# In the middle of a long convolution, GpSimd folds products that TensorE summed, and the last routing steps move

## The chip, the core and the metric

The kernel runs on one core of one Trainium2 chip. A core has TensorE (matmuls into PSUM), VectorE, ScalarE and GpSimd (elementwise work; GpSimd reaches SBUF only) and SyncE, called SP, which here only issues DMAs. The metric is the time of one execution on the device in microseconds, the median of three runs.

## The reference

A gated long convolution over 4 sequences ("blocks" below) of 11456 tokens and 128 channels, then a mixture of 8 experts, each token sent to one of them.

```python
h_filt = (np.maximum(pos_emb @ w1, 0.0) @ w2) * np.exp(-0.01 * pos)[:, None]
y = irfft(rfft(x * v, 2 * S) * rfft(h_filt, 2 * S))[:, :S]   # causal convolution along the sequence
x = (x * y).reshape(B * S, D)
logits = x @ w_gate + modality_bias[modality_id]
e_idx = np.argmax(logits, axis=1)
gate_w = softmax(logits)[np.arange(N), e_idx]
out[mask] = gate_w[mask, None] * (np.maximum(x[mask] @ w1[e], 0.0) @ w2[e])   # for each expert e
```

## The kernel before

**The convolution** is a two-step transform. After the filter has been transformed once (its spectra go to DRAM as `hs`), each of the four blocks has an *outer stage* and a *middle*. The outer stage of block b has 16 steps: it multiplies x by v and transforms them (forward), and for block b - 1 it does the inverse transform, the multiplication by x, and the routing: logits, `choice` (maximum, exponential, first best expert as a one-hot array `oh` and its running count `sc`), and `send`, which in spite of its name makes only the ranks (row numbers `ix` within each expert's region) from matmuls of `oh` and `sc`. Routing goes in octets `o` of 0 to 7, one every two steps. `store` writes an octet's finished rows from SBUF (`xo`) to DRAM (`xr`), two DMAs of 365.6 KB on SP; `places` writes the row numbers once all are known.

**The middle** of a block has 23 groups of four rows of the spectrum, `A` (the last has two). For group g, `spectrum` is TensorE's second transform (line 602) into a pair of PSUM banks, of which there are two; `products` has VectorE multiply it with the filter's spectra: two half-size products into `more` (line 619), two full ones into `part` (line 626). GpSimd combines `more` (lines 621, 622); one subtraction on `part` (line 630, GpSimd up to group 4, VectorE after) and one addition (line 631, GpSimd) follow. `inverse` sums on TensorE, for its two output blocks: two terms of `p` (which is `part[0]`) for block 0, and the same two and two of `more` for block 1 (line 650). ScalarE copies the result into `A`. Two groups go together: spectrum and products of groups 2k and 2k + 1, and then the inverse of the pair before. SP loads for each group its constants `c_b` (for `spectrum`) and `c_c` (for `inverse`) and the spectra `hs`, into rings of three places; a load waits until its place has been read.

**The order** of instructions on TensorE, ScalarE, VectorE and SP is that of the program; `steps` builds lists of steps, and `joined` writes out by hand how the end of an outer stage goes over into the middle. In its list, `mid[0]` has groups 4 and 5 (spectrum, products), `mid[1]` the inverse of 2 and 3, `mid[2]` groups 6 and 7, and so on; each step also holds the loads of one group. SP is such a queue, too: a DMA that waits holds up all that are written behind it. GpSimd's order is left to the framework's planner.

**Rows sent.** Each row of a routed block must go to its expert's region in DRAM, `xs`. `fetch` (SP) loads a block's row numbers, and `send_rows(n)` sends n columns of 128 rows by indirect DMAs of GpSimd (line 267); every fifth column needs a load of rows on ScalarE's queue. A block has 90 columns. They are sent in the outer stages (`paced`: after an instruction of VectorE), in the middles, and among the expert tiles.

**The experts.** 82 tiles of 512 rows and 22 of 256 follow (of the last five, only as many as are needed), with two matmul layers in chunks of 128 hidden channels, each in three matmuls of split precision; GpSimd scatters the results (line 1216).

Of the kernel before, what the change touches and what calls it, by code (L numbers as in the profile page):

```python
# [33 lines left out]
PU = 64 + HALF  # L34
# [4 lines left out]
NG = -(-N1 // G)  # L39
# [138 lines left out]
def hyena_moe_kernel(ctx: ExitStack, tc: tile.TileContext, a: dict, out: bass.AP,  # L178
# [46 lines left out]

    scatters, waiting, finale = [], [], []
    order_dep = mybir.DependencyInfo(mybir.DependencyClass.NoSync, mybir.DependencyReason.DATA)
# [25 lines left out]
    def fetch(b):  # L253
# [3 lines left out]
        waiting.extend((b, c) for c in range(NR // D))  # L257

    def send_rows(n, behind=None, wait=None):


        for _ in range(min(n, len(waiting))):
            b, c = waiting.pop(0)
            if c % RC == 0:
                rows_back(b, c // RC + 1, act)
            ix, src = to_t[b % 2][:, c:c + 1], back_t[(b * NB + c // RC) % 3][:, c % RC]
            s = pool.indirect_dma_start(  # L267
                out=xs, out_offset=bass.IndirectOffsetOnAxis(ap=ix, axis=0), in_=src,
                in_offset=None, bounds_check=E * R - 1, oob_is_err=False)
            free_rows(scatters, s)  # L270
            if behind is not None:
                tc.add_manual_dep(ins_of(s), behind.name, order_dep, reason="order of issue")
            if wait is not None:
                tc.add_manual_dep(ins_of(s), wait.name, sync_dep, reason="pace")
# [85 lines left out]
    with ExitStack() as cv:  # L360
# [80 lines left out]
        def forward_stages(b):  # L441
# [7 lines left out]
            def product(q):  # L449

                u = kept[q, "u"]
                s = dve.tensor_mul(u, u, kept.pop((q, "v")))
                paced(s, 2)

# [116 lines left out]
        def middle_stages(b):  # L571
# [36 lines left out]
            def products(g):  # L608
# [13 lines left out]
                pool.tensor_add(more[:, 0, 1], more[:, 0, 1], more[:, 1, 0])  # L622
                if g == 6 and b > 0:
                    fetch(b - 1)
                for i in range(2):
                    dve.tensor_mul(  # L626
                        part[i], z[:, :, i].unsqueeze(1).broadcast_to([D, 2, n, 2, D]),
                        h[:, 0].unsqueeze(3).broadcast_to([D, 2, n, 2, D]))
                p = part[0]
                (pool if g <= 4 else dve).tensor_sub(p[:, 0], p[:, 0], part[1][:, 1])  # L630
                s = ins_of(pool.tensor_add(p[:, 1], p[:, 1], part[1][:, 0]))  # L631
                if 4 < g < NG - 2:
                    send_rows(1 + (g % 3 == 0), s)
                k["p"], k["m"] = p, more[:, 0]

            def inverse(g):
# [4 lines left out]
                for q in range(n):  # L641
                    for blk in range(2):
                        terms = [(p[:, c, q, blk], c) for c in range(2)]
                        if blk:
                            terms += [(more[:, c, q], c) for c in range(2)]
                        for i, (t, c) in enumerate(terms):
# [18 lines left out]
        def inverse_stages(b):  # L665
# [15 lines left out]
            def transform(q):  # L681
# [3 lines left out]
                for c in range(2):  # L685
                    for blk in range(2):
# [7 lines left out]
                paced(dve.tensor_mul(xo_of(b, q // 2)[:, :, q % 2, :, 0:D], four(y),  # L694
                                     four(kept.pop(q))))

# [14 lines left out]
        def route_stages(b):  # L711
# [55 lines left out]
            def choice(o):  # L767
                i = b * NO + o
                xo = xo_of(b, o)
                lg = kept.pop(o)  # L770
# [5 lines left out]
                act.activation(ex[:, 0:E], dl, AF.Exp)  # L776
                oh, sc = oh_t[i % 2], sc_t[i % 2]
                sco = score[0:PU]
                dve.scalar_tensor_tensor(sco[:, 0:E], dl, 0.0, fst, op0=ALU.is_ge, op1=ALU.mult)
                mb = rt.tile([PU, NC], F32, tag="mb", name="mb")  # L780
                dve.tensor_reduce(mb, ec(sco), axis=AX.X, op=ALU.max)
                dve.tensor_tensor(oh[0:PU], sco[:, 0:E], wide(mb), op=ALU.is_equal)
                dve.tensor_tensor_scan(
# [36 lines left out]
            def places(o):  # L820
                if o == NO - 1:
                    for blk in range(2):
                        at = xi[b].rearrange("(k n x) -> k n x", k=2, n=HALF)
                        sp.dma_start(at[blk], ix_all[64 * blk:64 * blk + HALF].rearrange("p w m -> p (w m)"))

            return turn, logits, logits_turn, shift, biased, choice, send, store, places

# [6 lines left out]
        def outer_steps(b):  # L834
# [3 lines left out]
            if b > 0:  # L838
                load_x, turn, itransform = inverse_stages(b - 1)
                rturn, logits, lturn, shift, biased, choice, send, store, places = route_stages(b - 1)  # L840
                todo = {
# [24 lines left out]
            if 0 < b < nb:  # L866
                for name in ("half", "logits", "lturn", "shift", "biased", "choice", "send", "store", "places"):
                    later[b, name] = lambda f=todo[name]: f(NQ - 1)
                    todo[name] = but_last(todo[name], 1)
                todo.pop("places")  # L870
# [8 lines left out]
        def joined(b, seq):  # L879
# [5 lines left out]
            if b == 0:  # L885
# [9 lines left out]
                    + do("shift", "half", "products0", "spectrum1", "logits", "load_h2", "load3",  # L895
                         "products1", "spectrum2", "lturn", "load_c1", "products2",
                         "inverse0", "load4", "load_c2", "spectrum3", "biased", "choice",
                         "inverse1", "load5", "load_c3", "store", "products3")
                    + mid[:1] + do("send") + keep + mid[1:2] + do("places") + mid[2:])

# [117 lines left out]
    def experts(lo, hi):  # L1018
# [209 lines left out]
        for at in range(len(work) + 6):  # L1228
# [8 lines left out]
            if lo == 0 and at >= FL + len(finale) + 2 and len(waiting) <= RC and not fetched:  # L1237
                fetched.append(fetch(nb - 1))
            if lo == 0 and at % 3 == 0:
                send_rows(1)  # L1240
# [66 lines left out]
```

## Time and profile before

| | |
|---|---|
| median of 3 runs | 2106.36 us (2105.53 to 2107.07) |
| the profiled execution | 2104.89 us, span 2102.7 us |
| busy share of the span | TensorE 97%, VectorE 80%, GpSimd 60%, ScalarE 57% |
| mean granted clock of TensorE | 0.992 of full speed |

In the profile PE is TensorE, PEld its weight loads, DVE VectorE, ACT ScalarE, POOL GpSimd, and SPq the DMA issues of SP; a line number is that of the kernel. The span goes from the first to the last instruction. The filter and the first forward stage take the first 149 us, the middles lie at 149 to 257, 382 to 496, 622 to 736 and 861 to 975 us, the outer stages between them and until 1062, and the experts after that. Busy shares are means over these stages; what bounds a stage is read from its own rows.

### The profile page before, as it was taken

To read this page: it belongs to the slowest core of one execution; us is meant where nothing else is said; L and a number is where in the kernel's file an instruction comes from. 1 tells how busy PE (TensorE), PEld (TensorE's weight loads), DVE (VectorE), ACT (ScalarE), POOL (GpSimd) and SP (SyncE) were. 2 spreads that over 40 slices of the span, in tenths; PEclk is the share of its full clock that TensorE was granted. 3 is DMA by queue.
4 is the path that set the end of the run, shared out by engine and by line. 5 is a ranking of instruction groups with operands and counts; after the bars stand their busy time and mean duration, and the time that the engine had idled before them with its cause. 6 is when DMAs were issued, how large, how long until landed. Compare 5 with 4: busy or idle time off the path is not lost. (4 is left out here: it accounts for less than half of the span.)

```text
span 2102.7 us, 50304 instructions
## 1 busy us (share of the span) xinstructions
PE 2037.7 (97%) x18162; PEld 1671.1 (79%) x18162; DVE 1680.5 (80%) x2692; ACT 1191.8 (57%) x2162; POOL 1251.2 (60%) x1337
## 2 busy tenths in 40 slices
PE   8989999899999999899999999999999999999996
PEld 8888877688767877687668888888888888888896
DVE  2348767896779867897887899988989999899885
ACT  4642266225652266324666666666666666666674
POOL 0207500597658866687746667777876465555553
PEclk9999999999999999999999999999999999999998
DMA  9577777687888789785798455665665554454310
GB/s 322 222 275 239 250 222 248 201 288 282 294 279 262 257 288 318 254 270 189 216 279 256 89 122 121 131 137 120 135 132 111 110 107 99 94 100 97 78 41 26
DMA packets 509590, 397.55 MB, mean 189 GB/s; under 512 B 372697, under 2 KB 406317, under 8 KB 509337
## 3 DMA queue, kind: packets, MB, share of 16 engines
q1 hardware_dynamic: 472889, 312.26, 53.1%
q0 software_dynamic: 26496, 59.36, 7.9%
q10 hardware_dynamic: 9952, 22.67, 3.8%
q8 instruction: 145, 2.38, 0.5%
q14 instruction: 108, 0.88, 0.1%
HBM read 290.58 MB, written 103.96 MB: 188 GB/s over the span
## 5 line engine op out<-in xcount | busy, mean ns | idle before, releaser
L1167 DVE SCALAR_TENSOR_TENSOR hl<-ph,hh 128x512 fp32r<-128x512 f32 x724 | 485.5, 680 | 101.2 <-ACT hh L1166 93.7
L1166 ACT ACTIVATE hh<-ph 128x512 fp32r<-128x512 f32 x724 | 425.1, 598 | 213.7 <-PE ph L1163 203.2
L267 POOL DMA_INDIRECT xs<-back,to x360 | 388.0, 1078 | 184.8 <-issue 65.5
L1216 POOL DMA_INDIRECT out<-ot,idx x362 | 395.0, 1091 | 140.4 <-issue 112.2
L1163 PE MATMUL ph<-xl,wh 128*128 128x512 f32 (+1 forms) x792 | 296.4, 374 | 4.5 <-DVE xl L1148 4.4
L1161 PE MATMUL ph<-xh,wh 128*128 128x512 f32 (+1 forms) x792 | 298.8, 377 | 1.1 <-ACT xh L1147 1.1
L1162 PE MATMUL ph<-xh,wl 128*128 128x512 f32 (+1 forms) x792 | 294.8, 372 | 1.0 <-DVE wl L1116 1.0
L1184 PE MATMUL po<-hh,wh 128*128 128x512 f32 (+1 forms) x792 | 294.8, 372 | 0.0
L1186 PE MATMUL po<-hl,wh 128*128 128x512 f32 (+1 forms) x792 | 294.3, 372 | 0.0
L1185 PE MATMUL po<-hh,wl 128*128 128x512 f32 (+1 forms) x792 | 294.0, 371 | 0.0
L655 ACT COPY A<-pw 128x512 f32<-128x512 f32 x180 | 96.0, 584 | 328.9 <-PE pw L650 328.9
L626 DVE TENSOR_TENSOR part<-pz,rings 128x1024 f32<-128x1024 f32 (+1 forms) x184 | 211.5, 1189 | 2.5 <-POOL part L631 2.5
L650 PE MATMUL pw<-rings,part 64*128 64x128 f32 x2880 | 200.6, 278 | 1.4 <-ACT A L655 1.4
L650 PEld LDWEIGHTS pw<-rings,part 64*128 64x128 f32 x2880 | 179.3, 190 | 19.7 <-issue 14.8
L602 PE MATMUL pz<-A,rings 128*64 128x256 f32 x1440 | 172.1, 389 | 18.9 <-issue 14.5
L464 PE MATMUL s<-fwd,seq 128*64 128x90 f32 x4096 | 170.8, 243 | 5.9 <-issue 4.2
L1163 PEld LDWEIGHTS ph<-xl,wh 128*128 128x128 f32 x792 | 149.6, 189 | 33.0 <-DVE xl L1148 5.8
L464 PEld LDWEIGHTS s<-fwd,seq 128*64 128x64 f32 x4096 | 161.3, 137 | 13.2 <-issue 4.9
L1162 PEld LDWEIGHTS ph<-xh,wl 128*128 128x128 f32 x792 | 149.7, 189 | 26.4 <-DVE wl L1116 1.3
L1161 PEld LDWEIGHTS ph<-xh,wh 128*128 128x128 f32 x792 | 149.6, 189 | 26.0 <-ACT xh L1147 1.3
L1184 PEld LDWEIGHTS po<-hh,wh 128*128 128x128 f32 x792 | 149.2, 188 | 26.0 <-issue 0.7
L1186 PEld LDWEIGHTS po<-hl,wh 128*128 128x128 f32 x792 | 149.2, 188 | 25.8
(191 smaller groups left out, 3606.8 us busy)
## 6 DMA issues: line engine op xcount, KB each, us to landing
rings<-hs SPq DMA_DIRECT2D x88, 512.0 KB
seq<-in_u SPq DMA_DIRECT2D x64, 512.0 KB
seq<-in_v SPq DMA_DIRECT2D x64, 512.0 KB
seq<-in_x SPq DMA_DIRECT2D x64, 512.0 KB
xr<-xo SPq DMA_DIRECT2D x64, 365.6 KB
rings<-in_c_b SPq DMA_DIRECT2D x88, 256.0 KB
rings<-in_c_c SPq DMA_DIRECT2D x88, 256.0 KB
back<-xr ACTq DMA_DIRECT2D x68, 325.0 KB
```

The source lines that it names most:

```text
L267: s = pool.indirect_dma_start(out=xs, out_offset=bass.IndirectOffsetOnAxis(ap=ix, axis=0), in_=src, in_offset=None, bounds_check=E * R - 1 ...
L464: pe.matmul(v[64 * c:64 * c + 64, blk, j], u[:, blk, 4 * h + j], fwd[:, c], start=True, stop=True)
L650: pe.matmul(pw[par][:, to:to + D], t[at], k["c"][at, q, c], start=i == 0, stop=i == len(terms) - 1)
L1161: pe.matmul(p, k[0, "h"][:, f:f + D], k["xh"], start=True, stop=False)
L1162: pe.matmul(p, k[0, "l"][:, f:f + D], k["xh"], start=False, stop=False)
L1163: pe.matmul(p, k[0, "h"][:, f:f + D], k["xl"], start=False, stop=True)
L1166: act.activation(hh, ph, AF.Relu)
L1167: dve.scalar_tensor_tensor(hl, ph, 0.0, hh.bitcast(F32), op0=ALU.max, op1=ALU.subtract)
L1184: pe.matmul(po, k[1, "h"][:, f], hh[:, t], start=g == 0, stop=False)
L1185: pe.matmul(po, k[1, "l"][:, f], hh[:, t], start=False, stop=False)
L1186: pe.matmul(po, k[1, "h"][:, f], hl[:, t], start=False, stop=g == NCH - 1)
L1216: s = pool.indirect_dma_start(out=out, out_offset=bass.IndirectOffsetOnAxis(ap=k["idx"][:, j:j + 1], axis=0), in_=ot[:, j, :], in_offset=N ...
```

## The change

- **Fold.** In groups 4 to 19 of block 0 and 10 to 19 of the other blocks, GpSimd adds `more[:, 0, 0]` to the block-1 half of `p[:, 0]` (256 elements a partition), and `inverse` leaves that term out. The last three groups and the first ones are not folded.
- **Who subtracts.** GpSimd does the subtraction on `part` in the first groups (below 4 in block 0, below 10 in the others) and in even groups up to 18; VectorE in the rest.
- **Rows.** The middle sends no rows any more, but for two after its last group. A block's `fetch` is made at group 15 or by `send_rows`, as soon as the block is stored and no more than five columns wait. In exchange every second `product` sends a column more, and every second `inverse` of the last outer stage; among the expert tiles one goes out in every second chunk of the first 12 tiles and then in three of eight.
- **The last two octets' routing.** The ranks of octet 6 move from the end of the outer stage to the place ahead of `mid[0]`. `choice` of octet 7 is split into `best` (maximum, difference, exponential, first best) behind `mid[0]`, and `chosen` (one-hot array, counts, gate) behind `mid[2]`; `store` follows `chosen`; the ranks of octet 7 come behind `mid[4]`, and `places` behind `mid[5]`. `biased` and the products of group 3 move ahead.

```diff
+    def fetch_next():
+        if stored and len(waiting) <= RC:
+            fetch(stored.pop(0))
     def send_rows(n, behind=None, wait=None):
+        fetch_next()
...
-                paced(s, 2)
+                paced(s, 2 + (q % 2 == 0))
...
-                if g == 6 and b > 0:
-                    fetch(b - 1)
+                if g == NG - 8:
+                    fetch_next()
...
-                p = part[0]
-                (pool if g <= 4 else dve).tensor_sub(p[:, 0], p[:, 0], part[1][:, 1])
-                s = ins_of(pool.tensor_add(p[:, 1], p[:, 1], part[1][:, 0]))
-                if 4 < g < NG - 2:
-                    send_rows(1 + (g % 3 == 0), s)
-                k["p"], k["m"] = p, more[:, 0]
+                p, early, late = part[0], g < (4 if b == 0 else 10), g >= NG - 3
+                by_pool = early or (g % 2 == 0 and not late)
+                (pool if by_pool else dve).tensor_sub(p[:, 0], p[:, 0], part[1][:, 1])
+                pool.tensor_add(p[:, 1], p[:, 1], part[1][:, 0])
+                k["p"], k["m"] = p, {c: more[:, 0, c] for c in range(2)}
+                if not early and not late:
+                    pool.tensor_add(p[:, 0, :, 1], p[:, 0, :, 1], k["m"].pop(0))
+                if g == NG - 1:
+                    send_rows(2)
...
-                            terms += [(more[:, c, q], c) for c in range(2)]
+                            terms += [(m[:, q], c) for c, m in more.items()]
...
-                                     four(kept.pop(q))))
+                                     four(kept.pop(q))), 1 + (b == nb - 1 and q % 2))
...
             def choice(o):
+                best(o)
+                chosen(o)
...
+                    if b < nb - 1:
+                        stored.append(b)
...
-                    todo[name] = but_last(todo[name], 1)
+                    todo[name] = but_last(todo[name], 3 if name == "send" else 1)
+                later[b, "ranks"] = lambda: send(NO - 2)
+                later[b, "best"], later[b, "chosen"] = lambda: best(NO - 1), lambda: chosen(NO - 1)
...
-                         "products1", "spectrum2", "lturn", "load_c1", "products2",
-                         "inverse0", "load4", "load_c2", "spectrum3", "biased", "choice",
-                         "inverse1", "load5", "load_c3", "store", "products3")
-                    + mid[:1] + do("send") + keep + mid[1:2] + do("places") + mid[2:])
+                         "products1", "spectrum2", "lturn", "load_c1", "biased", "products2",
+                         "inverse0", "load4", "load_c2", "spectrum3", "products3",
+                         "inverse1", "load5", "load_c3", "ranks")
+                    + mid[:1] + do("best") + mid[1:3] + do("chosen", "store") + mid[3:5]
+                    + do("send") + keep + mid[5:6] + do("places") + mid[6:])
...
-            if lo == 0 and at % 3 == 0:
+            if lo == 0 and c % (2 if i < 12 else 3) == 0:
                 send_rows(1)
```

## Rows read from the trace of the kernel before

**Rows 1.** Stretches: length; busy PE, PEld, DVE, ACT, POOL; clock; DMA share; GB/s.

```profile
368.00:420.00 52.00, 45.87 (x567) 34.50 (x565) 42.49 (x71) 14.93 (x28) 26.06 (x30) 0.97 0.66 199
420.00:473.00 53.00, 53.00 (x738) 43.94 (x736) 50.33 (x60) 13.40 (x26) 49.47 (x53) 1.00 0.87 289
788.00:841.00 53.00, 53.00 (x704) 39.32 (x701) 38.02 (x74) 36.01 (x67) 34.23 (x37) 1.00 0.92 320
1200.00:1400.00 200.00, 200.00 (x884) 165.77 (x883) 180.67 (x279) 135.80 (x240) 146.89 (x152) 1.00 0.59 125
```

**Rows 2.** Timeline of PE, settled middle: start, us, instruction, idle before.

```profile
690.31 3.67 PE L602 MATMUL pz<-A,rings 128*64 128x256 f32 x32
...
695.36 1.06 PE L650 MATMUL pw<-rings,part 64*128 64x128 f32 x16
696.25 0.61 PE L650 MATMUL pw<-rings,more 64*128 64x128 f32 x8
696.69 1.06 PE L650 MATMUL pw<-rings,part 64*128 64x128 f32 x16
...
699.47 3.67 PE L602 MATMUL pz<-A,rings 128*64 128x256 f32 x32
```

**Rows 3.** Timeline of VectorE (DVE), settled middle.

```profile
705.66 1.28 DVE L619 TENSOR_TENSOR more<-pz,rings 128x512 f32<-128x512 f32 x2
...
709.23 0.69 DVE L630 TENSOR_TENSOR part<-part 128x512 f32<-128x512 f32 x1
```

**Rows 4.** Timeline of GpSimd (POOL) in early groups, where it sends no rows.

```profile
407.48 0.72 POOL L622 TENSOR_TENSOR more<-more 128x256 f32<-128x256 f32 x1
408.17 1.27 POOL L630 TENSOR_TENSOR part<-part 128x512 f32<-128x512 f32 x1
409.40 1.26 POOL L631 TENSOR_TENSOR part<-part 128x512 f32<-128x512 f32 x1
```

**Rows 5.** Groups by line, GpSimd, 170 to 250 us (block 0): busy, mean ns.

```profile
L631 POOL TENSOR_TENSOR part<-part 128x512 f32<-128x512 f32 x18 | 30.7, 1704 | 12.4 <-DVE part L626 12.3
```

**Rows 6.** Timeline of GpSimd among the expert tiles: two sends.

```profile
1303.45 0.98 POOL L267 DMA_INDIRECT xs<-back,to  x1 [0.30 <-issue]
1304.73 0.98 POOL L267 DMA_INDIRECT xs<-back,to  x1 [0.30 <-issue]
```

**Rows 7.** Timeline of PE, entry of the middle of block 1.

```profile
382.31 1.95 PE L602 MATMUL pz<-A,rings 128*64 128x256 f32 x16 [0.86 <-ACT A L467]
...
389.22 1.95 PE L602 MATMUL pz<-A,rings 128*64 128x256 f32 x16 [1.19 <-issue]
...
391.71 1.16 PE L650 MATMUL pw<-rings,part 64*128 64x128 f32 x16
...
404.29 2.69 PE L602 MATMUL pz<-A,rings 128*64 128x256 f32 x16 [3.00 <-issue]
...
407.25 1.87 PE L650 MATMUL pw<-rings,part 64*128 64x128 f32 x16
...
414.45 3.67 PE L602 MATMUL pz<-A,rings 128*64 128x256 f32 x32
```

**Rows 8.** Timeline of VectorE, entry of block 1: `biased`, and the products after `choice`.

```profile
395.95 0.29 DVE L764 TENSOR_TENSOR lg<-lt,lg 109x128 f32<-109x128 f32 x1
...
400.66 1.27 DVE L619 TENSOR_TENSOR more<-pz,rings 128x512 f32<-128x512 f32 x2
```

**Rows 9.** Timeline of SP's DMA issues, entries of blocks 1 and 3.

```profile
400.78 1.78 SPq L797 DMA_DIRECT2D xr<-xo  x2
402.66 1.56 SPq L577 DMA_DIRECT2D rings<-in_c_b  x1
...
899.11 0.43 SPq L577 DMA_DIRECT2D rings<-in_c_b  x1
```

**Rows 10.** Stretch behind that store in block 1, columns as in the first group.

```profile
402.00:407.00 5.00, 2.71 (x18) 1.60 (x19) 5.00 (x6) 0.00 (x0) 4.07 (x5) 0.84 0.82 201
```

**Rows 11.** Timeline of PE, entry of block 3.

```profile
905.12 1.95 PE L602 MATMUL pz<-A,rings 128*64 128x256 f32 x16 [0.99 <-DMA rings<-in_c_b]
```

More of the change, by code (lines that the diff above doesn't have):

```diff
@@ L224, in hyena_moe_kernel @@
     sc_t = [cst.tile([D, E, NC], BF16, name=f"sc{i}") for i in range(2)]
-    scatters, waiting, finale = [], [], []
+    scatters, waiting, finale, stored = [], [], [], []
     order_dep = mybir.DependencyInfo(mybir.DependencyClass.NoSync, mybir.DependencyReason.DATA)
@@ L767, in choice, with best @@
             def choice(o):
-                i = b * NO + o
-                xo = xo_of(b, o)
+                best(o)
+                chosen(o)
+            def best(o):
                 lg = kept.pop(o)
@@ L776, in choice @@
                 act.activation(ex[:, 0:E], dl, AF.Exp)
-                oh, sc = oh_t[i % 2], sc_t[i % 2]
                 sco = score[0:PU]
@@ L781, in choice, with chosen @@
                 dve.tensor_reduce(mb, ec(sco), axis=AX.X, op=ALU.max)
+                kept[o] = mb
+            def chosen(o):
+                i = b * NO + o
+                xo = xo_of(b, o)
+                mb = kept.pop(o)
+                ex, sco = powers[0:PU], score[0:PU]
+                oh, sc = oh_t[i % 2], sc_t[i % 2]
                 dve.tensor_tensor(oh[0:PU], sco[:, 0:E], wide(mb), op=ALU.is_equal)
@@ L824, in places @@
                         sp.dma_start(at[blk], ix_all[64 * blk:64 * blk + HALF].rearrange("p w m -> p (w m)"))
-            return turn, logits, logits_turn, shift, biased, choice, send, store, places
+                    if b < nb - 1:
+                        stored.append(b)
+            return turn, logits, logits_turn, shift, biased, choice, send, store, places, best, chosen
         def every_other(f):
@@ L839, in outer_steps @@
                 load_x, turn, itransform = inverse_stages(b - 1)
-                rturn, logits, lturn, shift, biased, choice, send, store, places = route_stages(b - 1)
+                rturn, logits, lturn, shift, biased, choice, send, store, places, best, chosen = route_stages(b - 1)
                 todo = {
```

## Prediction

> **What bounds the kernel now.** I read the stretches first, then the instructions of one stretch, then the place where a stretch begins. In the middle of a block (420 to 473 us) TensorE is busy for all of 53 us, VectorE for 50.3 and GpSimd for 49.5: three engines close to one another, and a change of one of them counts only as far as the next allows [rows 1]. In the outer stage and among the expert tiles TensorE is busy throughout as well, with VectorE and GpSimd further behind [rows 1]. Where a middle begins (368 to 420 us) it is busy for 45.9 of 52 us, at a granted clock of 0.97: six microseconds of idle time at the first of three such entries, where the block before is still being routed [rows 1].
>
> In the settled middle, one pair of groups takes 9.16 us from one 32-instruction spectrum to the next [rows 2]. It has the spectrum, 3.6 us, and the inverse of the pair before, four runs of 24 instructions (16 on `part`, 8 on `more`) 1.33 us apart, so 55.6 ns an instruction [rows 2]. VectorE's four products of a group take 3.57 us from the first to the subtraction behind them, and the subtraction 0.69 [rows 3]: 8.5 us a pair, so VectorE follows TensorE.
>
> **1. The fold.** A matmul of the inverse is two instructions here: 24 calls of a full group, 48 instructions [rows 2]. Without the term `more[:, 0]` there are 20 calls, so 8 instructions go per group, 16 per pair, 0.89 us. A pair would take 9.16 - 0.89 = 8.27 us. Folded are groups 4 to 19 of block 0 and 10 to 19 of the three others: 46 groups, 23 pairs, 20.5 us if TensorE stays the bound.
>
> Does GpSimd allow it? Per pair it now has four half-size operations on `more`, two additions on `part`, two folds of 256 elements (no row shows a fold; a `more` operation has its size and operands, and I take its price), and one subtraction for the even group. Start to start, without sends, a half-size operation takes 0.69 us and a full-size one 1.23 [rows 4]. 6 x 0.69 + 3 x 1.23 = 7.83 us. The odd group's subtraction on VectorE reads two SBUF tiles beside a GpSimd operation; in block 0, where this happens in each group, the addition takes 1.70 us instead of 1.27 [rows 4, 5]. One such meeting a pair: 8.26 us. That is TensorE's 8.27, so GpSimd is the engine to fear. The Trainium skill (GPSIMD Engine Reference, 1. Specifications) names the same: GpSimd shares its SBUF interfaces with VectorE and suffers under instructions with two SBUF inputs; the row agrees, with 0.43 us. VectorE comes to 2 x 3.57 + 0.69 = 7.8 us, with one subtraction less [rows 3]. Bounds of a pair's gain: 0.89, and 0.76 with a second half meeting beyond TensorE's time (8.4). I take 0.80: 23 x 0.80 = **-18.5 us** (17.5 to 20.5).
>
> **2. The entry of the middle, blocks 1 to 3.** Counted from the first spectrum at 382.31, the seventh starts 32.1 us later, at 414.45 [rows 7]. TensorE idles 1.19 us ahead of the third and 3.00 ahead of the sixth spectrum; each waits for the PSUM pair that VectorE's products must release [rows 7]. After the second idle time the clock has dropped, and the sixth spectrum takes 2.69 instead of 1.95, the inverse run after it 1.87 instead of 1.16, so 1.45 us more [rows 7]. The reason is VectorE: `biased` and `choice` stand ahead of the fourth product, 395.95 to 400.66 [rows 8], 4.7 us. The change puts the first rank (one wait of VectorE for TensorE) and the choice behind products, whose PSUM pairs are then released in time: fourth product at +13, fifth and sixth from +18 to +25, all ahead of the spectra that need their pairs. So the seventh spectrum would start at about 32.1 - 1.2 - 3.0 - 1.45 - 0.3 (one rank's three matmuls come later) = 26.2, and 5.9 us would be won in each block.
>
> But `store` moves too, and it is two DMAs on SP, which issues in the written order. It waits for the last instruction of `chosen`, and behind it stand the loads of group 9 and all later ones. From the seventh spectrum at 26.2: its PSUM pair is full at 28.1, the products of groups 6 and 7 take 2 x 3.57 us of VectorE [rows 3], and `chosen` (the second half of a choice, 1.8 us by its share of [rows 8]) ends at 37.0. TensorE needs `c_b` of group 9 one pair and half a spectrum after the seventh, at 26.2 + 9.16 + 1.87 = 37.2 [rows 2]. At that time its load has not been issued. In the kernel before, the same store began at 400.78 and the next load at 402.66 [rows 9]; from 402 to 407 the queues moved 5.0 us x 201 GB/s = 1.0 MB [rows 10], which is the store's two times 365.6 KB and that load's 256 KB. A `c_b` behind a store has landed about 6.2 us after the store's start. That gives 43.2 for group 9 and 6 us of idle TensorE. A second row: in block 3 the load of group 9 was issued at 899.11, behind other loads, and TensorE waited 0.99 us for it until 905.12, 6.0 us after the issue [rows 9, 11]. The Trainium skill (DMA: Bandwidth & Descriptors, Queues, rings and completion order) says that each DMA engine consumes a ring's descriptors in order and that SP has one ring on each; so a load can't pass a store of the same issuer. By that the 6.2 us stand; a load that could pass the store would be there 3.7 us sooner (0.75 MB at 201 GB/s), and the stall would be 2.3 us.
>
> Group 9's spectrum started at 32.1 + 9.16 + 1.87 = 43.2 in the kernel before [rows 2, 7], and 1.0 later in block 3 [rows 11]. So the entry ends where it ended, and what is new comes on top: a fallen clock after 6 us of idle time (1.45 us after 3 us; up to 3 after 6, an estimate from this row) and a rank's matmuls, 0.3. Per block +1.8 to +3.3, in block 3 a microsecond less. Sum for three: **+5.5 us** (3.5 to 9). Without the stall it would be 3 x -5.9 = -17.7.
>
> `send` moved two pairs later and `places` behind it hold SP again, for VectorE's four small operations; the loads behind them are wanted some 9 us later, as before. Nothing for these.
>
> **3. The rows sent elsewhere.** A send takes GpSimd 1.28 us from start to start [rows 6]. By the code, the three middles sent 20, 21 and 21 rows; now 2 each. 56 sends move: 8 into each of the outer stages 2, 3 and 4 (4.5 a step for 4, and 3.5 for 3), 32 among the expert tiles. In an outer stage GpSimd is busy 34 of 53 us and hides them; the DMA engines are at 0.92 there [rows 1], and half a send a step adds 2 or 3 hundredths. A tile has 48 matmuls, 48 x 200 / 884 = 10.9 us [rows 1]; four sends and four output scatters are 8 x 1.28 = 10.2 us of GpSimd, 11.5 with the full-size product that tiles 9 to 11 add (1.26, as [rows 4]): it falls some 2 us behind there, and four buffers cover that. `fetch`, now in the outer stage, puts two loads on SP that wait for rows sent a step earlier. From nothing to 3 us: **+1**.
>
> **Sum.** -18.5 + 5.5 + 1 = -12 us. The profiled execution took 2104.9 us (span 2102.7), the median is 2106.4; 2106.4 - 12 = **2094 us**.
>
> **Rivals.** *The stall is short.* If `c_b` of group 9 comes within 2 us of need, the entry's gain is kept: -18.5 - 17.7 + 6 (three times 2 us) + 1 = 2077; with no stall 2071; with half of it and the fallen clock 2084. For it speaks that the queue is otherwise empty when the store goes out; against it are the slow 201 GB/s and the two rows of 6 us. 22 in 100.
>
> *GpSimd sets the pace (slower).* If a meeting with VectorE costs 0.43 us not once but three times a pair, a pair takes 7.83 + 1.3 = 9.13 us, the fold gives back 0.7 us in all, and +5.5 + 1 is left: 2112. It is slower than now by over 0.2% from 9.06 us a pair on. At 8.7 the time is 2102. Against it: VectorE has one subtraction a pair left, and its products read PSUM. The skill's rule, above, makes this case. 10 in 100, half of it on the slow side.
>
> *The sends come to the surface.* DMA engines near full in the outer stages, or GpSimd too late among the tiles: some 0.15 us a step over 48 steps, 7 us: 2100. 8 in 100.
>
> *As forecast*, 2089 to 2099: 55 in 100. For mishaps that I don't see, 5.
>
> **Chances and range.** 0.2%, 4.2 us, is about what a measurement tells from no change. Below 2102.2 lie the forecast, the short stall, the sends, and some of the GpSimd case: 0.87. Within 0.2%: 0.07; slower: 0.06. Range 2073 to 2102: it leaves out the case without a stall and the slow end.
>
> **What the profile after will show.** Right: `pw<-rings,more` 368 instructions fewer, 1072 for 1440; pairs of about 8.3 us in the folded groups; no 3 us gap ahead of the sixth spectrum, and instead a gap of about 6 us ahead of the tenth (group 9), ended by a DMA of `c_b`, SP's `xr` store standing right ahead of that load. Wrong: no such gap (then the time is near 2071), or pairs that stay at 9 us with TensorE waiting for GpSimd's `part`.

## The result, and the profile after

The kernel after takes **2125.1 us** (median of 4, 2123.4 to 2129.0) for 2106.0 before on the same chip: 1.0094 times the time, interval 1.0077 to 1.0112. It is slower by 0.9%; 2094 was forecast. The profiled execution has a span of 2121.6 us, 18.9 more than before. In the profile after, some lines have other numbers: `spectrum` is 608 (602 before), `inverse` 659 (650), a send 273 (267), `store` 815 (797), the load of `c_b` 583 (577), the fold 641, the addition behind the subtraction 638 (631), the subtraction 637 (630).

Stretches of after; columns as in [rows 1]. In order: the entry of block 1, a settled folded stretch, an outer stage, the last outer stage, the expert tiles.

```profile
363.00:437.00 74.00, 63.26 (x793) 48.38 (x793) 56.44 (x85) 19.52 (x38) 43.15 (x50) 0.93 0.62 199
437.00:475.00 38.00, 37.69 (x526) 31.25 (x524) 36.56 (x41) 9.61 (x18) 35.77 (x40) 1.00 0.76 248
788.00:841.00 53.00, 51.95 (x704) 39.27 (x703) 38.07 (x73) 36.02 (x67) 41.32 (x40) 1.00 0.91 320
979.00:1081.00 102.00, 86.76 (x599) 54.67 (x598) 70.19 (x156) 60.40 (x110) 70.12 (x72) 0.94 0.64 190
1200.00:1400.00 200.00, 200.00 (x885) 165.68 (x884) 181.76 (x290) 133.67 (x239) 150.92 (x157) 1.00 0.58 126
```

The folded stretch and the expert tiles are full, as forecast. TensorE idles at the entry and, over 15 of 102 us, in the last outer stage. There the kernel before had this row (976 to 1063 us), 3 us idle of 87; it did not stand among [rows 1]:

```profile
976.00:1063.00 87.00, 83.93 (x599) 53.02 (x599) 69.19 (x156) 60.49 (x110) 59.25 (x65) 1.00 0.70 206
```

PE's timeline in after, block 1: the entry from its first spectrum on; then the last pair that isn't folded (433.03 to 442.19, 9.16 us) and the first folded one (from 442.19 to 450.46, 8.27 us; answers to [rows 2, 7]).

```profile
377.10 1.95 PE L608 MATMUL pz<-A,rings 128*64 128x256 f32 x16 [0.86 <-ACT A L473]
...
402.44 3.67 PE L608 MATMUL pz<-A,rings 128*64 128x256 f32 x32
...
411.60 1.95 PE L608 MATMUL pz<-A,rings 128*64 128x256 f32 x16
422.19 3.68 PE L608 MATMUL pz<-A,rings 128*64 128x256 f32 x16 [8.64 <-DMA rings<-in_c_b]
...
433.03 3.67 PE L608 MATMUL pz<-A,rings 128*64 128x256 f32 x32
...
442.19 3.67 PE L608 MATMUL pz<-A,rings 128*64 128x256 f32 x32
...
450.46 3.67 PE L608 MATMUL pz<-A,rings 128*64 128x256 f32 x32
```

SP's issues there (answers to [rows 9]):

```profile
402.78 0.38 SPq L597 DMA_DIRECT2D rings<-in_c_c  x1
414.94 1.78 SPq L815 DMA_DIRECT2D xr<-xo  x2
416.81 1.56 SPq L583 DMA_DIRECT2D rings<-in_c_b  x1
```

No idle time stands ahead of the sixth and seventh spectra any more, and the seventh starts 25.3 us after the first. But SP issues nothing from 403.2 to 414.9; then `store` goes out, and the load of group 9 behind it. TensorE stands for 8.64 us (8.73 and 8.59 in blocks 2 and 3), and the spectrum that ends the wait takes 3.68 us instead of 1.95. From the first spectrum to that of group 10 it is 55.9 us; before, the same way took 50.5 (382.31 to 432.77).

ScalarE in the last outer stage of after. ACTq is its DMA queue; `back` is the buffer (three of them) from which GpSimd sends rows, loaded ahead for five sends.

```profile
1008.30 0.58 ACT L699 COPY y<-py 128x512 f32<-128x512 f32 x1 [1.20 <-PE py L696]
1014.81 0.33 ACTq L251 DMA_DIRECT2D back<-xr  x1
1015.24 0.52 ACT L751 COPY lT<-pl 128x436 f32<-128x436 f32 x1 [6.35 <-DMA xs<-back,to]
...
1071.54 0.33 ACTq L251 DMA_DIRECT2D back<-xr  x1
1071.96 0.89 ACT L741 COPY rings<-xT 128x872 f32<-128x872 f32 x1 [5.05 <-DMA xs<-back,to]
...
1079.01 0.33 ACTq L251 DMA_DIRECT2D back<-xr  x1
1079.38 0.52 ACT L751 COPY lT_late<-pl 128x436 f32<-128x436 f32 x1 [6.05 <-DMA xs<-back,to]
```

Each of these three times ScalarE stands at a load of `back` until an earlier send has landed. Counted in order, five sends to a buffer, the sends that the three loads had to wait for last are these:

```profile
1008.23 1.01 POOL L273 DMA_INDIRECT xs<-back,to  x1 [0.39 <-DVE ix L835]
...
1065.87 0.98 POOL L273 DMA_INDIRECT xs<-back,to  x1 [0.30 <-DVE oh L800]
...
1075.37 1.63 POOL L273 DMA_INDIRECT xs<-back,to  x1 [0.34 <-issue]
```

The third started 2 us after ScalarE had begun to wait (1073.33): GpSimd was behind with its sends. TensorE's waits behind these copies, the last at the first expert matmul:

```profile
1015.81 1.19 PE L757 MATMUL lt<-ident,lT 128*109 128x128 f32 x4 [5.79 <-ACT lT L751]
...
1072.90 0.93 PE L747 MATMUL pl<-rings,wg 128*32 128x436 f32 x6 [1.61 <-ACT rings L741]
1080.96 0.79 PE L1184 MATMUL ph<-xh,wh 128*128 128x512 f32 x1 [6.54 <-ACT xh L1170]
```

**Where the time went**, by stage. A stage is counted on PE's timeline from its first spectrum, its first transposition of `wt` or the first expert matmul to the start of the next one. The outer stages carry the block's number: 2 and 3 ("second and third" in the expectations) and the last, 4, send rows; that of block 1 sends none. Differences after minus before, us: middle of block 0 -6.05; middles of blocks 1 to 3 +2.34, +2.10, -0.36; outer stages 2 and 3 +2.49 and +1.31; last outer stage **+15.50** (86.61 to 102.11); outer stage 1 0.0; expert tiles +0.73; ahead of the first spectrum +0.84. Sum 18.9.

### The profile page after: what moved, and what is told of

Same layout as the page of the kernel before. It is cut to its first block, busy times and chain, and to the rows that moved or that the text cites. A ratio compares the mean times of both kernels' runs of the same rounds, so it can differ in the third digit from the quotient of the medians.

```text
span 2121.6 us, 49660 instructions
## 1 busy us (share of the span) xinstructions
PE 2025.8 (95%) x17794; PEld 1653.4 (78%) x17794; DVE 1671.6 (79%) x2655; ACT 1187.3 (56%) x2162; POOL 1329.8 (63%) x1420
## 5 line engine op out<-in xcount | busy, mean ns | idle before, releaser
L1184 PEld LDWEIGHTS ph<-xh,wh 128*128 128x128 f32 x792 | 149.5, 189 | 31.4 <-ACT xh L1170 6.8
L608 PEld LDWEIGHTS pz<-A,rings 128*64 128x64 f32 x1440 | 102.0, 140 | 88.3 <-issue 34.5
L1185 PEld LDWEIGHTS ph<-xh,wl 128*128 128x128 f32 x792 | 149.6, 189 | 25.3
```

What stands on the lines that cost most here:

```text
L1184: pe.matmul(p, k[0, "h"][:, f:f + D], k["xh"], start=True, stop=False)
L1185: pe.matmul(p, k[0, "l"][:, f:f + D], k["xh"], start=False, stop=False)
```

## The experiments

They ran on four other chips, and there the kernel before itself took 2138 to 2171 us, on one of them 2164 at one time and 2138 later. So each is set against before on its own chip, and stages are compared. Expectations with absolute times (the first four) had the first chip in mind. Stage lengths in us, from one profiled execution of each, on PE's timeline as above; the ratio is that to before on the same chip, with its interval:

| kernel | chip | middle 0 | middles 1-3, mean | outer 2 and 3, mean | last outer | experts | ratio |
|---|---|---|---|---|---|---|---|
| before | first | 108.1 | 114.7 | 124.9 | 86.6 | 1039.9 | 1 |
| after | first | 102.1 | 116.0 | 126.8 | 102.1 | 1040.6 | 1.0094 |
| store_later | second | 103.2 | 106.3 | 150.1 | 101.7 | 1101.9 | 1.0133 (1.0054-1.0211) |
| three_rows | second | 102.4 | 118.5 | 147.5 | 92.3 | 1104.4 | 1.0308 (1.0232-1.0384) |
| finer_back | second | 102.4 | 117.0 | 152.5 | 109.4 | 1068.5 | 1.0263 (1.0189-1.0336) |
| both | second | 103.5 | 107.8 | 146.4 | 90.0 | 1113.8 | 1.0106 (1.0024-1.0189) |
| before_again | third | 106.9 | 115.3 | 134.4 | 88.8 | 1055.6 | one run |
| after_again | third | 102.2 | 117.5 | 144.7 | 101.6 | 1063.0 | 1.0299 (1.0252-1.0346) |
| calm_store | third | 102.4 | 107.5 | 136.6 | 97.1 | 1107.8 | 1.0179 (1.0128-1.0230) |
| old_entry | third | 103.3 | 110.5 | 148.0 | 102.7 | 1065.2 | one run |
| sends_moved | fourth | 106.7 | 114.6 | 147.9 | 105.6 | 1107.4 | 1.0236 (1.0184-1.0289) |
| lean | fourth | 102.3 | 114.7 | 135.4 | 93.1 | 1085.8 | 0.9963 (0.9915-1.0011) |
| both_again | fourth | 103.2 | 108.1 | 150.4 | 92.8 | 1122.1 | 1.0142 (1.0074-1.0211) |
| both_third | fifth | 103.1 | 107.4 | 146.3 | 89.0 | 1083.0 | 1.0078 (1.0052-1.0104) |
| fold_first | second | 102.2 | 114.8 | 134.6 | 87.5 | 1052.5 | 0.9975 (0.9955-0.9995) |

The middles hardly depend on the chip; outer stages 2 and 3 and the expert tiles, in which rows are sent, do. Outer stage 1, in which none are sent, took 124.9 to 125.0 us in every one of these profiles.

**store_later** is after with `store` behind the loads of groups 9 and 10:

```diff
-                    + mid[:1] + do("best") + mid[1:3] + do("chosen", "store") + mid[3:5]
-                    + do("send") + keep + mid[5:6] + do("places") + mid[6:])
+                    + mid[:1] + do("best") + mid[1:3] + do("chosen") + mid[3:5]
+                    + do("store", "send") + keep + mid[5:6] + do("places") + mid[6:])
```

> The changed kernel with one difference: the last octet's store stands behind the loads of groups 9 and 10 on SP, not ahead of them. Theory (the store holds SP's queue): the 8.6 us of idle TensorE ahead of group 9's spectrum go in all three entries, and with each about 2.7 us of fallen clock; 3 x 11.3 = 34 us, so 2125 becomes about 2091. Rival (the load of group 9 is late because the DMA engines are slow there, wherever the store stands): a gap of 5 us or more stays, 2115 or more.

The middles of blocks 1 to 3 are 9.3, 9.3 and 10.5 us shorter than in after (34 us had been expected for the three). SP's queue there, and the spectra of groups 8 and 9, which now run as one row without a wait:

```profile
404.22 0.33 SPq L583 DMA_DIRECT2D rings<-in_c_b  x1
...
414.74 1.78 SPq L815 DMA_DIRECT2D xr<-xo  x2
```

```profile
411.39 3.67 PE L608 MATMUL pz<-A,rings 128*64 128x256 f32 x32
```

So the place of `store` cost 29 us in the three entries. The whole was still slower than before: the loss sits in the other stages, and 2091 us was missed by far.

**three_rows** is after with the last outer stage back at three columns a step, and the rest among two more tiles:

```diff
-                                     four(kept.pop(q))), 1 + (b == nb - 1 and q % 2))
+                                     four(kept.pop(q))))
-            if lo == 0 and c % (2 if i < 12 else 3) == 0:
+            if lo == 0 and c % (2 if i < 14 else 3) == 0:
```

> The changed kernel, but the last outer stage sends 3 columns a step again, not 3.5; the 8 columns that are left go out among the expert tiles (one in every second chunk for 14 tiles instead of 12). Theory (too many sends there: GpSimd falls behind, ScalarE's queue stands at the load of the next rows until old rows are out, and its copies come late): the last outer stage takes 87 to 90 us instead of 102, the time is about 2112. Rival 1 (the fetch that now falls into this stage holds SP): it stays at about 2122. Rival 2 (8 more columns among the tiles cost as much as they save): 2125.

The last outer stage is 92.3 us (87 to 90 expected), 9.4 less than in store_later on the same chip, whose sends are those of after. The whole missed its number by far, since on this chip the other stages with sends were 20 us and more longer than on the first.

**finer_back** is after with five buffers of three columns instead of three of five (`RC = 3`, `back_t[... % 5]`), so that ScalarE's load comes longer after the sends that read its buffer. `RC` also says how few columns may wait when the next block is fetched, now three.

> The changed kernel with 3.5 columns a step as it is, but rows are loaded in five buffers of 3 columns instead of three buffers of 5, so that a load waits for rows sent ten columns earlier, not six. Theory (ScalarE's queue is what carries GpSimd's backlog to TensorE): the waits of ScalarE for sent rows in the last outer stage, 5 to 6 us each, mostly go, 2112 to 2116. Rival (GpSimd's backlog delays TensorE by another way, the bias sums it makes for the routing): the stage still takes 100 us, 2125.

The waits of ScalarE for `DMA xs<-back` come to 1.9 us in the whole profile (31.4 in after), but the last outer stage takes 109.4 us, more than the 100 of its rival. So on this chip it is not these waits that make the stage long. Two other waits of ScalarE stand there instead, 4.60 and 4.61 us, which the profile puts down to "remote" (see the last section). The expert tiles were shorter, 1068.5 against 1101.9 in store_later.

**both** has the edits of store_later and three_rows; it ran on three chips.

> Both differences together, the store behind the loads of groups 9 and 10, and 3 columns a step in the last outer stage. If the two losses are separate places, they add: 2125 - 34 - 13 = 2078, 28 us faster than the kernel before. If one of them only uncovers the other, about 2091 or more.

> The kernel with the store behind the loads and the last outer stage at three rows a step, once more, for another chip. Theory (on a chip where ScalarE's second copy of a step is not held up, only the two causes count): middles at 107 to 109.5 us and 104.6 for block 3, second and third outer stages 126 to 128, the last one 87 to 91, the whole 0.985 to 0.991 times before. Rival (the loss in the outer stages and expert tiles is the moved sends' own on every chip): second and third outer stages over 135 us, the whole over 1.000.

> The kernel with the store behind the loads and the last outer stage at three rows a step, a third time, for the chance of a chip on which TensorE's signals are not held up while GpSimd sends rows (as in the first profiles, where ScalarE's second copy of a step followed its matmuls at once). Theory (on such a chip the two causes are all of the loss): the kernel before near 2106 us there, this one at 2072 to 2088, 0.984 to 0.991 times before. Rival (the moved sends lose on every chip): before at 2140 us or more and this one over 1.005 times it, or before near 2106 and this one over 0.995 times it.

The middles came as expected and the last outer stage nearly so (107 to 108 and 89 to 93 us); outer stages 2 and 3, at 146 to 150 us, did not. On none of the three chips did it beat before, so the rivals of both_again and both_third held. Whether it would on the first chip wasn't measured.

**before_again** and **after_again** are the two kernels unchanged.

> The kernel before itself, unchanged, for its stage lengths on the chip of this batch. On the first chip its three middles of blocks 1 to 3 took 114.3, 114.4 and 115.3 us, its second and third outer stages 124.9 and 125.0, its last one 86.6 and its expert tiles 1039.9. Theory (the first four runs lost time to a slower chip, not to their own order): on a slower chip these outer stages and the expert tiles are longer here too, by 20 us and more each, and the middles are not. Rival (what those runs lost in the outer stages came from the sends that the change puts there): all its stages are as on the first chip.

> The kernel after itself, unchanged. Theory: 1.008 to 1.012 times the time of before on the same chip, its middles of blocks 1 to 3 at 116.7, 116.5 and 115.0 us whatever the chip, its last outer stage some 15 us longer than that of before. Rival (its loss is a trait of the first chip): the same time as before, within 0.3%, with a last outer stage no more than 5 us longer.

Both theories held in part. The ratio, 1.0299, is far above the 1.008 to 1.012 expected. Before itself has outer stages 10 us longer there, and expert tiles 16 us longer; but after loses another 10 us in each of outer stages 2 and 3, 12.8 in the last and 7 in the expert tiles.

**calm_store** is store_later with no extra sends in any outer stage, and four a tile in the first 27 tiles.

> The kernel after with the store behind the loads of groups 9 and 10, and with no more sends in the outer stages than the kernel before had there; what is left over goes among the first 27 expert tiles, four a tile. Theory (the store ahead of the loads, and the extra sends of the outer stages, are the two causes of the loss): middles near 107.4, 107.2 and 104.5 us, outer stages as in the kernel before on the same chip within 1.5 us, the whole 0.984 to 0.990 times before (2072 to 2085 us on the first chip). Rival 1 (the sends only change their place and come to the surface among the expert tiles): the expert tiles 8 us or more longer than in the kernel before, the whole 0.990 to 1.000. Rival 2 (the outer stages are longer for another reason than their number of sends, for instance the late fetch): the last outer stage 8 us or more longer than in the kernel before.

Outer stages 2 and 3 fall to 136.6 us, 2.2 above before. The expert tiles take 52 us more: the sends only changed their place. Rival 1 holds, and the whole lost more than it said. The last outer stage is 8.3 us longer than in before_again, which meets the number of rival 2; but 6.49 of that is a deadline that this kernel had made tight. The first tile's rows wait for the 180th send, which started at 1061.79, and their transposition on TensorE stands ahead of the first expert matmul, with which the stage ends:

```profile
1067.08 1.08 PE L1160 MATMUL px<-ident,x 128*128 128x128 f32 x4 [6.49 <-DMA x<-xs]
```

**old_entry** is after with the entry of before (`choice` and rank whole, `store` ahead of the load of group 6).

> The kernel after with the entry of the middle in the order of the kernel before (choice and rank whole, the store ahead of the load of group 6, three rank sends as before); the fold and the moved sends stay. Theory (the store behind group 7's products is what costs, the reorder of the products itself gains some 4 us a block): middles of blocks 1 to 3 near 111 us, 5 to 6 us shorter than in the kernel after and 3 to 4 longer than with the store moved behind the loads. Rival (the reorder gains nothing, and only the fold shortened the middles): 107 to 108 us, as with the store moved.

Its middles are 21.3 us shorter in sum than those of after_again on the same chip, and 9.0 longer than those of calm_store. So the reorder, with the store behind the loads, gains 3 us a block, and the store behind group 7's products loses 10.

**sends_moved** is before with the moved sends alone; no fold, and the old entry.

> The kernel before with one part of the change alone: the rows are sent where the kernel after sends them (two a middle, more in the outer stages and among the expert tiles, the fetch in the outer stage); the fold and the new entry are left out. Theory (the moved sends are the larger part of the loss, some 19 us on the first chip): the three middles within 1.5 us of before's, the last outer stage 10 to 16 us longer than before's, the second and third 1 to 10 us longer, the whole 1.006 to 1.02 times before. Rival (what the prediction said, 0 to 3 us): the whole within 0.2% of before, the last outer stage no more than 2 us longer.

The middles stay as in before, so the sends had cost nothing there. The whole is 2.4% slower (0.6 to 2 expected), so the stages that take the sends lose; before itself has no profile on this chip. This is the part that the prediction had priced at +1. What the loss looks like here, in its outer stage 2: matmuls of the forward transform (`s`) end at 565.5, and ScalarE's copy of their second half starts at 568.36. GpSimd sends rows in between, and what TensorE does next comes late. In after on the first chip the copy of a second half follows the first after 0.48 us (at 564.89).

```profile
562.47 2.01 POOL L273 DMA_INDIRECT xs<-back,to  x1 [1.00 <-DVE xo L700]
562.77 2.70 PE L470 MATMUL s<-fwd,seq 128*64 128x90 f32 x64
...
564.53 0.76 ACT L473 COPY A<-s 128x720 f32<-128x720 f32 x1 [1.08 <-PE s L470]
...
564.79 0.98 POOL L273 DMA_INDIRECT xs<-back,to  x1 [0.30 <-DVE score L786]
...
566.08 0.99 POOL L273 DMA_INDIRECT xs<-back,to  x1 [0.31 <-issue]
...
567.37 0.98 POOL L273 DMA_INDIRECT xs<-back,to  x1 [0.30 <-issue]
568.36 0.76 ACT L473 COPY A<-s 128x720 f32<-128x720 f32 x1 [3.07 <-PE wt L684]
...
570.33 0.22 PE L821 MATMUL pr<-oh,both 109*128 109x128 bf16 x1 [1.11 <-ACT rings L685]
```

**lean** is before with the fold in block 0 alone, the entry of store_later, and the sends left in the middles, `fetch` four groups later.

> The kernel before with its sends left in the middles, the fold in block 0 alone (where no rows are sent), and the new entry with the store behind the loads of groups 9 and 10; the fetch comes some four groups later, once the rows waiting are five or fewer. Theory (fold and entry gain, and what loses is the store's place and the moved sends): middle of block 0 at 102 us, of blocks 1 to 3 at 109.5 to 111.5 (before: 114.3 to 115.6), outer stages and expert tiles as in before, the whole 0.990 to 0.994 times before on any chip. Rival (GpSimd, with its sends crowded into fewer groups, sets the pace of the middle): middles of blocks 2 and 3 at 114 us or more, the whole 0.996 or more.

Middle 0 came as expected. The middles 1 to 3 took 115.2, 116.8 and 112.0 us: from group 8 on, three pairs a block take 9.2 to 13.5 us there, where before mostly has 9.16. Its sends are crowded into fewer groups; that this is the cause wasn't tested. The ratio can't be told from 1. Among the expert tiles lean also sends more densely in the first six.

**fold_first** is before with the fold in block 0 alone, where the middle sends nothing:

```diff
-                p = part[0]
-                (pool if g <= 4 else dve).tensor_sub(p[:, 0], p[:, 0], part[1][:, 1])
+                p, fold = part[0], b == 0 and 4 <= g < NG - 3
+                by_pool = g % 2 == 0 if fold else g <= 4
+                (pool if by_pool else dve).tensor_sub(p[:, 0], p[:, 0], part[1][:, 1])
...
+                if fold:
+                    pool.tensor_add(p[:, 0, :, 1], p[:, 0, :, 1], k["m"].pop(0))
...
-                            terms += [(more[:, c, q], c) for c in range(2)]
+                            terms += [(m[:, q], c) for c, m in more.items()]
```

> The kernel before with the fold in block 0 alone, where no rows are sent; entry, store, fetch and sends are the kernel before's. Theory (the fold is a gain by itself, 0.77 to 0.89 us a pair over eight pairs, and nothing else of the change is needed for it): the middle of block 0 at 102 to 103.5 us for 107 to 108, all other stages as in before, the whole 4 to 6 us faster, 0.9970 to 0.9985 times before. Rival (a gain in the middle is given back where the engines wait for transfers in the outer stage behind it): the first outer stage or the middle of block 1 longer by 3 us or more, the whole within 0.1% of before.

It is **faster than the kernel before**, by a quarter of a percent: 2132.5 for 2138.5 us, 0.9975 (0.9955 to 0.9995). A pair of its block 0:

```profile
210.09 3.67 PE L602 MATMUL pz<-A,rings 128*64 128x256 f32 x32
...
218.36 3.67 PE L602 MATMUL pz<-A,rings 128*64 128x256 f32 x32
```

It takes 8.27 us. The middle is 4.7 us shorter than in before_again, and the other stages are as there.

## Why the prediction was wrong

**1. The fold: right, with one wait that wasn't foreseen.** A folded pair takes 8.27 us (442.19 to 450.46) for 9.16, as forecast from 16 instructions less. The 46 folds on GpSimd took 758 ns in the mean (groups by line); the half-size operation that stood in for one had 0.72 [rows 4].

```profile
L641 POOL TENSOR_TENSOR part<-part,more 128x256 f32<-128x256 f32 x46 | 34.9, 758 | 0.7 <-DVE part L637 0.7
```

In the folded stretch GpSimd is busy for 35.8 of 38 us and TensorE for 37.7, so GpSimd did not set the pace there. The meeting of the two engines showed on the other side: GpSimd's addition did not become longer (1.27 us in the mean from 437 to 475 us; the prediction took 1.70), but VectorE's subtraction did (median 1.02 us in after, 0.69 in before). Once, in block 0, it took 4.68 us, while GpSimd worked without a break until 196.28, and ended at 196.83:

```profile
192.15 4.68 DVE L637 TENSOR_TENSOR part<-part 128x512 f32<-128x512 f32 x1
...
195.00 1.28 POOL L638 TENSOR_TENSOR part<-part 128x512 f32<-128x512 f32 x1
...
203.85 1.95 PE L608 MATMUL pz<-A,rings 128*64 128x256 f32 x16 [1.51 <-issue]
```

TensorE then stood twice, for 0.58 and 1.51 us, and two of the eight folded pairs of block 0 took 9.0 and 10.0 us. Every kernel with the fold in block 0 has this subtraction, at 4.66 to 4.70 us, and those without have none above 2.61; that GpSimd's work holds it up is read from these rows, not tested. Middle 0 became 6.05 us shorter, but 1.1 of that lie in a pair that isn't folded (groups 2 and 3, with the inverse behind them): 11.1 us in before, 10.0 in after and in before_again. In blocks 1 to 3 the way from the spectrum of group 10 to the end of the middle became 3.1, 4.0 and 4.5 us shorter, 11.6 in sum (on other chips, old_entry's middles are 12.5 us shorter in sum than those of sends_moved). Together 17.7; -18.5 was forecast, from 0.80 us a pair where a settled one gave 0.89.

**2. The entry: right in mechanism, too small.** The chain came as told: products earlier, the seventh spectrum at +25.3 (+26.2 forecast), `chosen` at +37.8 (+37.0), SP held by `store`, group 9's spectrum late, and a fallen clock after the idle time (0.93 in the entry's row). `c_b` of group 9 let TensorE go 7.25 us after the store's start (6.2 forecast), 5.4 after its own issue. The trace doesn't contradict what the Trainium skill (DMA: Bandwidth & Descriptors, Queues, rings and completion order) says of descriptors consumed in order on a ring, but the same section lets a later one finish its write first. Nor does the trace prove that a load can't pass a store: in block 3 of before a load with only loads right ahead of it took 6.0 us from its issue [rows 9, 11]. The stall is 8.64 us for 6, since TensorE wanted the load at +36.5 and had it at +45.1; 3.3 us of it had passed before SP issued the load. From that spectrum to the next it is 10.8 us, where before took 7.3: the slow spectrum (1.7), the rank and a slow inverse. From the first spectrum to that of group 10 the three middles grew by 5.5, 6.1 and 4.1 us on the first chip: the entry cost +15.7, where +5.5 stood, with 9 at the most. The rival of a short stall fell.

**3. The rows sent elsewhere: this step failed.** It stood at +1, with 3 at the most, and the stages that take the sends grew by 20.0 us on the first chip (2.49 + 1.31 + 15.50 + 0.73), enough by itself to turn the sign: -18.5 + 5.5 + 20 = +7. The sentence that failed is "In an outer stage GpSimd is busy 34 of 53 us and hides them". It priced all outer stages by the row of one, 788 to 841 us. The last outer stage has no forward transform: its 16 steps take 86.6 / 16 = 5.4 us each. In before, GpSimd was busy there for 59.25 of 87 us, and each of 46 sends leaves 0.3 us more that the row doesn't count [rows 6]: 73 us. After has 53 sends in this stage and comes to 70.12 + 53 x 0.3 = 86 us, all of the stage's former length. ScalarE stood for 6.35, 5.05 and 6.05 us where a load of `back` waits for sends, and TensorE behind it for 5.79, 1.61 and 6.54, which is 13.9 of its 15.2 us of idle time. The prediction's rival of sends coming to the surface named the mechanism at 7 us over all stages, with 8 in 100.

That the number of sends makes that stage long, on the other chips too, is shown by three_rows and by the kernel both, against store_later (92.3 and 90.0 for 101.7); the last two differ in nothing but where these rows are sent. In sends_moved, where fold and entry are left out, the stage takes 105.6 us. That ScalarE's wait for a buffer is the link is read from rows, not tested: it stands in this stage in store_later, after_again and sends_moved as well (2.9, 7.2 and 7.2 us in sum) and not in three_rows or both; but finer_back removed it without shortening the stage. The kernel both still takes 2.5 us more there than fold_first on that chip (87.5); the late `fetch` may be why, which wasn't tested. In all, on the first chip: -17.7 + 15.7 + 20.0, and 0.8 ahead of the first spectrum, make the 18.9.

## What to carry to other kernels

Work that is moved has to be priced in the stage that receives it, against that stage's own step, not by a row of a stage with the same name: the outer stage read from 788 to 841 us, of 7.8 us a step, had room for GpSimd on the first chip, the last one of 5.4 us a step had not. A DMA that is moved down a queue takes the loads behind it along; the move pays only if it is put behind those that the bound engine wants next (29 us here). And of a change in three parts, the part that gains may not need the others: the fold alone, in the one middle that sends nothing, was the only version that measurably beat the kernel before.

## What the runs showed of the hardware

A send costs its 1.28 us of GpSimd on each chip, but on the four other chips it cost other engines more. The kernel before took 124.9 us in the mean for outer stages 2 and 3 on the first chip and 134.4 on the third; its outer stage 1, without sends, took 125.0 on both. ScalarE's waits that the profile can't put down to an engine or a DMA of the kernel ("remote") are absent in the first profiles of before and after. They come to 10.3 us in before_again, and in sends_moved to 43.8 (ScalarE's waits: total us, times, longest):

```profile
ACT hh L1183 <- remote: 30.7, 16, 7.1
ACT A L473 <- remote: 11.5, 3, 4.2
```

In the kernel both (second chip), ScalarE stood for 11.4 us in the expert tiles while GpSimd issued sends and output scatters one after another, and TensorE for 10.1:

```profile
1153.52 0.40 PE L1186 MATMUL ph<-xl,wh 128*128 128x512 f32 x1
...
1163.37 0.60 ACT L1189 ACTIVATE hh<-ph 128x512 fp32r<-128x512 f32 x1 [11.43 <-remote]
...
1164.02 0.79 PE L1207 MATMUL po<-hh,wh 128*128 128x512 f32 x1 [10.10 <-issue]
```

The matmul that ScalarE's `hh` needs had ended at 1153.9. That such delays come while rows are sent is seen in many places; what holds TensorE's signal back, and why the first chip shows none of it, wasn't tested and stays open. One chip gave 2164 us for the kernel before at one time and 2138 at another, so it isn't a fixed trait of a chip either.

A send's row mostly ends 0.98 us after it starts, yet the three loads of `back` in the last outer stage of after went out 5.6, 4.7 and 2.0 us after the row of the send that they waited for had ended. The Trainium skill (Perfetto Trace Analysis, DMA Instruction — SWDGE (GPSIMD)) says that the profiler's end of such an instruction is the last written descriptor and not the moved data; these rows agree.
